# Attention and mixer in one stream: a transpose ahead of its scores, a rank product behind its slot's unit, and the last weight decode two slots later

## The chip, the cores and the metric

One core of a Trainium2 chip. The metric is the device time of one execution in microseconds (us). Engines as in the profile: PE (matmul), PEld (its weight loads, which overlap), DVE, ACT, POOL, SP (issues the transfers).

## What is computed

The output of a causal attention with decay feeds a token mixer of rank 32 and a channel network. B=8, 8 heads, S=576, D=64, width 512, inner width 2048:

```python
scores = scale * q @ k.T + (cum_i - cum_j), masked above the diagonal
attn   = softmax(scores);  o = attn @ v            # per head
x = o as (B, S, 512)
u = x + (x.T @ U @ V).T
out = u + relu(u @ w_ch1) @ w_ch2
```

`cum` is the running sum of log f. All of it is in float32 accuracy. A product is made of float32r parts: the high part is a rounded copy of an operand, the low part the rest; three products (high by high, high by low, low by high) make one.

## The kernel before

**Pairs and steps.** The 64 heads go as 32 pairs p=0..31, four to a batch. `step(t)` takes t=0..33; its ten slots s=0..9 overlap three pairs: p=t gets its scores, the pair before it (a) is transposed and multiplied by V, the pair before that (c) is scaled into x and split. Pairs 0 to 5 run their scores in float32 while the mixer's weights are decoded; from p=6 (`NF`) on in float32r.

**One pair.** Scores of the first head (`S_00` to `S_03`, L418 and L419) stand in slots 0 to 3, the last 64 rows of both heads (`St_0`, `St_1`, L472 and L473) in slots 4 and 5, those of the second head (`S_10` to `S_13`) from the end of slot 6 to slot 9. Each is followed by a maximum on DVE (L439, L477), which yields the bias `nm`, and an exponential on ACT (`P`, L449; `Ptl`, L487). One step later PE transposes `P` (L530; `T_00` to `T_02`, `T_v`, `T_10` to `T_12`), ACT copies the high part (`PTh`, L506), DVE subtracts for the low part (`PTl`, L509), and PE multiplies by V (L642; its operand `VS` is split by ACT at L203 and POOL at L208). Two steps later x is transposed and split (`xT`, `xh`, `xl`), and `ranks` multiplies it by U (`Tt`, L715), after which ACT and DVE copy `TS` (L718, L719, L722).

**Operands of the scores.** `G[0]` and `G[1]` hold q and k of the two heads for p of 6 and more. For each head three casts (L339) write the high parts, then L358 and L359 the low parts of k and of q; `St` reads both heads, its first product G0 alone, the other two G1. Normally ACT and POOL share this. In the pair that follows a mixing step (p=11, 15, 19, 23, 27, 31) all casts of G1 are POOL's.

**Mixer and network.** While attention runs, the steps with p=10, 14, 18, 22, 26 and 30 also run the mixing units of a finished batch: `H`, `Tu` (transposes of u, L780) and `Tv`. u's high part `uh` and low part `ul` are written from PSUM by ACT and DVE; for the last two `Tu` ACT copies the whole (`full`, L755), and POOL writes `uh` (L758) and `ul` (L759) from it. In other steps units of the network, `A` (12 matmuls, L832) or `B` (6 matmuls, L854), stand at the end of a slot, one to a slot as they are due.

**What sets the order.** The order of PE and SP is the order of the code. On ACT, DVE and POOL a scheduler orders the instructions of the attention part; `defer(phase, fn, slots)` says in which later slot, and in what place in it, an instruction is issued to the scheduler, and `behind(ins, kind)` orders one behind the newest of a kind. PSUM: the scores of p of 6 and more alternate between two buffers (`psS`), transposes between two (`psT`), units between two (`psF`); an instruction that writes a buffer waits for the last reader of what was in it.

**The decodes.** The weights come as integers that are decoded on the chip in 14 pieces u=0..13, `DECODES` gives step and slot. The last two (u=12, 13) are halved. The second half of u=13, which belongs to step 7, is issued 3 slots behind its first half, and its first instruction is ordered behind the newest score maximum (`newest["top"]`).

**What touches the change.** In slot 7: `score(p, 1, 1)`, that is `S_11`, stands ahead of `turn_p(a, 1, 1)`, that is `T_11`. In slot 8: `S_12`, `T_12`, `ranks(c)`, that is `Tt`, then the slot's unit.

Of the kernel before, what the change touches and what calls it, by code (L numbers as in the profile page):

```python
# [38 lines left out]
NF = 6  # L39
# [4 lines left out]
def tile_decay_attention_moe(ctx, tc, qk, v, f, U, V, w1, w2, out):  # L44
    nc = tc.nc
# [9 lines left out]
    newest = {}  # L55

    def behind(ins, kind):
        found = newest[kind]
        for x in found if isinstance(found, tuple) else (found,):
            tc.add_manual_dep(  # L60
                ins.ins, x.ins.name,
                mybir.DependencyInfo(mybir.DependencyClass.NoSync, mybir.DependencyReason.DATA), reason=f"order behind {kind}",
            )

    def decode(raw, a, h, l, eng, rows=slice(0, 128), keep=False, sub=nc.gpsimd, low=None, halves=(0, 1)):

        lo, hi = raw[..., 0].bitcast(U32), raw[..., 1]
        af, gf = a.bitcast(F32), hi.bitcast(F32)
        if 0 in halves:
            decode_words(a, af, hi, gf, eng, keep)
        if 1 in halves:
            third = nc.vector.tensor_scalar(hi, a, -0x800000, None, op0=ALU.bitwise_and)
            if 0 not in halves:
                behind(third, "top")
            nc.vector.scalar_tensor_tensor(gf, lo, 2.0**-52, gf, op0=ALU.mult, op1=ALU.mult)
            sub.tensor_tensor(af, af, gf, op=ALU.add)  # L80
            nc.scalar.copy(h, af)
            (low or sub).tensor_tensor(l[rows], af[rows], h.bitcast(F32)[rows], op=ALU.subtract)
# [167 lines left out]
    def decode_w(u, halves=(0, 1)):  # L250
        load_w(u)
        raw, a = staged[u]
        if 1 in halves:
            staged[u] = None
        kind, fc = UNITS[u]
        if kind == "w1":
            h, l = (x[:, fc].rearrange("p c f -> p (c f)") for x in (w1h, w1l))
        elif kind == "w2":
            h, l = w2h[:, fc], w2l[:, fc]
        elif kind == "V":  # L260
            h, l = VV, VV
        else:
            raw = raw.rearrange("p (c r) t -> p c r t", c=NM + 1)
            a = a.rearrange("p (c r) -> p c r", c=NM + 1)
            h, l = Us[:, :, 0:RK], Us[:, :, RK : 2 * RK]
        decode(raw, a, h, l, nc.scalar, slice(96, 128) if kind == "V" else slice(0, 128), keep=True, sub=nc.vector if u not in (0, LATE) else nc.gpsimd, low=nc.vector if 0 < u < LATE else nc.gpsimd, halves=halves)
        if u == len(UNITS) - 1 and 1 in halves:
            nc.gpsimd.memset(xn[NX - 1][64:128, NM, :], 0.0)

# [7 lines left out]
    def defer(phase, fn, slots=1):  # L277
        later.setdefault(now[0] + slots, []).append((phase, fn))
# [6 lines left out]
    def run_filler():  # L285
        w, fn = filler.pop(0)
        fn()
        return w
# [134 lines left out]
    def bank_s(p, name):  # L423

        scored[0] += 1
        if p < NF and scored[0] % 2:
            return psF.tile([P, 512], F32, tag="F", name=name)
        return psS.tile([P, 512], F32, tag="S", name=name)

    def score(p, j, i):  # L430
        z = st[p]
        w = P * (i + 1)
        ps = bank_s(p, f"S{p}_{j}{i}")
        c0 = AMAIN[j] + P * i
        qk_mm(ps[:, :w], p, c0, slice(0, w), True, True, j)
        col = 2 * i + j

        def top():
            ins = newest["top"] = nc.vector.tensor_tensor_reduce(  # L439
                ps[:, :w], ps[:, :w], mask[:, 512 - w : 512], scale=-SCALE, scalar=3.0e38,  # L440
                op0=ALU.add, op1=ALU.min, accum_out=z["nm"][:, col : col + 1],
            )
            if (j, i) == (0, 1) and "joined" in newest:
                behind(ins, "joined")

        def use():
            pt = sb2.tile([P, w], F32, tag=f"P{i}", name=f"P{p}_{j}{i}")
            z["P"][j].append(pt)
            ins = nc.scalar.activation(  # L449
                pt, ps[:, :w], AF.Exp, bias=z["nm"][:, col : col + 1], scale=-1.0, accum_out=z["sm"][:, col : col + 1]  # L450
            )
            if (j, i) == (0, 0):
                newest["exp"] = ins

        defer(0, top)
        defer(2, use)
# [3 lines left out]
    def score_tail(p, x):  # L460
        z = st[p]
        ps = bank_s(p, f"St{p}_{x}")
        cols = slice(hw * x, hw * x + hw)
        if p < NO:
            for j in range(2):
                qk_mm(ps[:, :hw], p, ATAIL[j], cols, j == 0, j == 1, j)
        elif p < NF:
            nc.tensor.matmul(ps[:, :hw], both_q, both_k[:, cols], start=True, stop=True)
        else:
            at = [slice(AOFF[j] + cols.start, AOFF[j] + cols.stop) for j in range(2)]  # L470
            for j in range(2):
                nc.tensor.matmul(ps[:, :hw], G[j][:, 0, ATAIL[j] : ATAIL[j] + P], G[j][:, 2, at[j]], start=j == 0, stop=False)  # L472
            nc.tensor.matmul(ps[:, :hw], G[1][:, 1, 0:P], G[1][:, 3, at[1]], start=False, stop=True)  # L473
        z["tl"].append(ps)

        def top():
            nc.vector.tensor_tensor_reduce(  # L477
                ps[:, :hw], ps[:, :hw], lean[:, hw * x : hw * x + hw], scale=-SCALE,
                scalar=3.0e38 if x == 0 else z["nm"][:, 8:9],
                op0=ALU.add, op1=ALU.min, accum_out=z["nm"][:, 8 + x : 9 + x],  # L480
            )

        def use():
            if x == 1:
                z["ptl"] = sb.tile([P, S], F32, tag="Ptl", name=f"Ptl{p}")
                for y in range(2):
                    newest["tail"] = nc.scalar.activation(  # L487
                        z["ptl"][:, hw * y : hw * y + hw], z["tl"][y][:, :hw], AF.Exp, bias=z["nm"][:, 9:10],
                        scale=-1.0, accum_out=z["sm"][:, 8 + y : 9 + y],
                    )  # L490

        defer(0, top)
        defer(2, use)

# [395 lines left out]
    def held(t):  # L890
        return 4 if t > MIX[-2] else 6
# [42 lines left out]
    LATE = 12  # L934
# [7 lines left out]
    def step(t):  # L942
        p = SEQ[t]
        a, c = (SEQ[t - x] if t >= x else None for x in (1, 2))
        ps_, pa, px = p is not None, a is not None, c is not None
        last, ending = t == LAST, t > LAST - 2
# [7 lines left out]
        for s in range(6 + 2 if last else SLOTS):  # L954
            when = now[0] + 1

            def at(phase, fn):
                later.setdefault(when, []).append((phase, fn))
# [31 lines left out]
            if (t, s) in DECODES:  # L990
                u = DECODES.index((t, s))

                steps = [lambda: load_w(u + (3 if u < 6 else 2)), lambda: decode_w(u)]
                if u < LATE:
                    for fn in steps if u < 8 else steps[::-1]:
                        at(6, fn)
                else:
                    at(6, lambda: decode_w(u, (0,)))
                    defer(6, lambda: decode_w(u, (1,)), 3)
                    defer(6, steps[0], 3)  # L1000
            run_later()
            if s == 4 and ps_ and p > NF:
# [12 lines left out]
            if ps_:  # L1015
                if s < 4:
                    score(p, 0, s)
                elif s < 6:
                    score_tail(p, s - 4)
                elif s > 6:  # L1020
                    score(p, 1, s - 6)
            if px and s == 0:
                values(c, 1)
# [5 lines left out]
                turn_small(a if pa else None, c if px else None)  # L1029
            if pa and s == 5:  # L1030
                turn_tail(a)
            if pa and 6 <= s < 9:
                turn_p(a, 1, s - 6)
            if pa and s == 7:
                values(a, 0)
            if px and s == (6 if last else 8):
                ranks(c)

            if mixing:
                for _ in range(2 if t == MIX[0] and s < 3 else 1):  # L1040
                    mixing.pop(0)[1]()
                for _ in range(1 if ending else (1, 1, 2, 1, 1)[s] if s < 5 else 0):
                    if filler:
                        run_filler()
            elif len(filler) > held(t) and s in ROOM:

                ahead = sum(x >= s for x in ROOM) + len(ROOM) * (min(m for m in MIX if m > t) - 1 - t)
                credit[0] += (len(filler) - held(t)) / max(ahead, 1)
                if credit[0] > 0.999 or t > LAST - 3:
                    credit[0] = max(credit[0] - 1, 0)  # L1050
                    run_filler()
            if ps_ and s == 6:
                score(p, 1, 0)
            if last and s == 7:
# [114 lines left out]
    with tc.manual_schedule(engines={ET.PE, ET.DVE, ET.Activation, ET.SP}):  # L1169
# [12 lines left out]
        h, t = ([fn for _, fn in x] for x in (mixing[0 : NM + 1], mixing[NM + 1 :]))  # L1182
# [622 lines left out]
```

## Time and profile before

| | |
|---|---|
| time, median of 3 runs | 1185.39 us (1185.22 to 1187.29) |
| the profiled execution's own time | 1184.63 us |
| its span | 1182.9 us |
| granted clock of TensorE | 0.999 of full speed |
| busy: PE, PEld, DVE, ACT, POOL | 99%, 91%, 76%, 64%, 50% |

The span is the stretch from the first to the last instruction of the profiled execution; busy shares are shares of it. Attention takes the first 660 us or so, the rest is the network and the last mixing.

### The profile page before, as it was taken

The page shows a single profiled execution, that of the slowest core. Times are in us where ns is not written, and L with a number is a line of the kernel's source. Part 1 is how long each engine was busy: PE and PEld are TensorE (multiplying, and loading weights), DVE is VectorE, ACT ScalarE, POOL GpSimd, SP SyncE. Part 2 cuts the span into 40 slices and gives each one's busy share as a digit, 9 for nine tenths or more (in the row PEclk, how much of TensorE's full clock was granted, in tenths as well). Part 3 has the DMA queues.
Part 4 walks back from the last instruction along what each step waited for, and adds up shares of the span by engine and source line. Part 5 has one row for each costly group of instructions (what it writes and reads, how often), then busy time and mean ns, then how long its engine had stood idle before and what let it go on. Part 6 is the DMA issues. An engine that isn't in the chain of part 4 may idle for free.

```text
span 1182.9 us, 24145 instructions
## 1 busy us (share of the span) xinstructions
PE 1168.8 (99%) x8348; PEld 1074.3 (91%) x8348; DVE 903.0 (76%) x2185; ACT 752.7 (64%) x2046; POOL 594.2 (50%) x668
## 2 busy tenths in 40 slices
PE   9999999999999999999999999999999999999998
PEld 5888899899999989989989987798999999999998
DVE  8987787677777677777686799967776767777675
ACT  8878786766868668867765577344454544544443
POOL 4216766547648458666563000024575555555554
PEclk9999999999999999999999999999999999999999
DMA  5754545536536536546443155352325335243411
GB/s 159 205 151 135 149 121 163 147 98 171 141 98 183 151 86 178 135 112 178 108 129 111 70 163 182 109 143 98 100 90 141 93 124 143 90 117 99 131 49 36
DMA packets 90610, 150.47 MB, mean 127 GB/s; under 512 B 12888, under 2 KB 50264, under 8 KB 88440
## 3 DMA queue, kind: packets, MB, share of 16 engines
q1 hardware_dynamic: 88856, 140.14, 40.4%
q0 software_dynamic: 1152, 8.39, 3.8%
q8 instruction: 66, 1.08, 0.4%
q14 instruction: 56, 0.46, 0.1%
q10 hardware_dynamic: 480, 0.40, 0.1%
HBM read 108.64 MB, written 35.93 MB: 122 GB/s over the span
## 4 chain that ended last, share of the span: by engine, by line
PE 85%; DVE 9%; ACT 3%; issue 1%; DMA 1%; POOL 1%; SPq 0%; DVEq 0%; POOLq 0%; ACTq 0%
PE N L1416 12%; PE B L854 11%; PE A L832 11%; PE A L1396 9%; PE B L1396 7%; PE V L642 6%; PE T L530 4%; PE S L418 3%; PE S L419 2%; PE O L1497 2%; PE B L1416 2%; PE V L607 2%; PE S L415 2%; PE Tt L715 2%; PE O L1260 1%
## 5 line engine op out<-in xcount | busy, mean ns | idle before, releaser
L208 POOL TENSOR_TENSOR hb<-xn,hb 128x256 fp32r<-128x256 f32 x136 | 111.6, 841 | 125.5 <-ACT hb L203 112.9
L449 ACT ACTIVATE P<-S,nm 128x128 f32<-128x128 f32 (+3 forms) x256 | 137.5, 539 | 58.0 <-DVE nm L439 56.0
L439 DVE CUSTOM_DVE_ANT_0 S<-S,mask 128x128 f32<-128x128 f32 (+3 forms) x256 | 125.4, 494 | 52.3 <-PE S L419 41.5
L832 PE MATMUL A<-uh,w1h 128*128 128x256 f32 (+1 forms) x384 | 119.7, 312 | 0.0
L832 PE MATMUL A<-ul,w1h 128*128 128x256 f32 (+1 forms) x384 | 113.6, 296 | 0.0
L832 PE MATMUL A<-uh,w1l 128*128 128x256 f32 (+1 forms) x384 | 113.4, 295 | 0.0
L203 ACT CAST hb<-xn 128x256 fp32r<-128x256 f32 x136 | 51.7, 404 | 84.6 <-DVE xn L1402 45.5
L339 POOL CAST G<-qk 64x576 fp32r<-64x576 f32 (+1 forms) x76 | 50.1, 668 | 89.2 <-PE S L419 56.8
L854 PE MATMUL B<-w2h,hh 128*128 128x512 f32 x216 | 88.2, 408 | 0.0
L509 DVE TENSOR_TENSOR PTl<-T,PTh 128x512 fp32r<-128x512 f32 (+1 forms) x156 | 78.1, 526 | 10.3 <-ACT PTh L506 9.9
L530 PE MATMUL T<-ident,P 128*128 128x128 f32 x544 | 85.3, 272 | 0.0
L854 PE MATMUL B<-w2l,hh 128*128 128x512 f32 x216 | 84.9, 393 | 0.0
L854 PE MATMUL B<-w2h,hl 128*128 128x512 f32 x216 | 84.7, 392 | 0.0
L358 POOL TENSOR_TENSOR G<-qk,G 64x576 fp32r<-64x576 f32 x52 | 74.7, 1437 | 10.8 <-issue 3.8
L1416 PE MATMUL N<-sw,hb 128*128 128x256 f32 x546 | 79.9, 282 | 0.0
L1416 PE MATMUL N<-b2h,hb 128*128 128x256 f32 x420 | 79.8, 282 | 0.0
L359 POOL TENSOR_TENSOR G<-qk,G 64x576 fp32r<-64x576 f32 x52 | 74.9, 1441 | 8.4 <-ACT G L339 7.5
L832 PEld LDWEIGHTS A<-uh,w1h 128*128 128x128 f32 x384 | 72.8, 190 | 0.9 <-DVE hl L837 0.4
L832 PEld LDWEIGHTS A<-uh,w1l 128*128 128x128 f32 x384 | 73.0, 190 | 0.5
L418 PE MATMUL S<-G 128*128 128x128 f32 x208 | 71.4, 348 | 2.0 <-ACT Ptl L487 0.9
L832 PEld LDWEIGHTS A<-ul,w1h 128*128 128x128 f32 x384 | 72.7, 189 | 0.0
L1416 PEld LDWEIGHTS N<-sw,hb 128*128 128x128 f32 x546 | 71.6, 190 | 0.0
(349 smaller groups left out, 3992.6 us busy)
## 6 DMA issues: line engine op xcount, KB each, us to landing
qk<-in_qk_dram SPq DMA_DIRECT2D x104, 288.0 KB
direct<-ud SPq DMA_DIRECT2D x48, 256.0 KB
sr<-in_w_dram SPq DMA_DIRECT2D x20, 512.0 KB
vr<-in_v_dram SPq DMA_DIRECT2D x32, 256.0 KB
ud<-uh SPq DMA_DIRECT2D x32, 256.0 KB
ud<-ul SPq DMA_DIRECT2D x32, 256.0 KB
accd<-ost SPq DMA_DIRECT2D x32, 256.0 KB
xn<-accd SPq DMA_DIRECT2D x8, 1024.0 KB
```

What stands on the lines that cost most here:

```text
L208: return leng.tensor_tensor(dl, src, dh.bitcast(F32), op=ALU.subtract)
L358: low = pin(el.tensor_tensor(g[oth, 2, cols], k[oth], gf[oth, 2, cols], op=ALU.subtract))
L359: last = pin(em.tensor_tensor(g[own, 1, cols], q[own], gf[own, 0, cols], op=ALU.subtract))
L418: nc.tensor.matmul(ps, G[j][:, 0, c0 : c0 + P], G[j][:, 2, cols], start=first, stop=False)
L439: ins = newest["top"] = nc.vector.tensor_tensor_reduce(ps[:, :w], ps[:, :w], mask[:, 512 - w : 512], scale=-SCALE, scalar=3.0e38, op0=ALU. ...
L449: ins = nc.scalar.activation(pt, ps[:, :w], AF.Exp, bias=z["nm"][:, col : col + 1], scale=-1.0, accum_out=z["sm"][:, col : col + 1])
L509: defer(2, lambda: nc.vector.tensor_tensor(dstl, src, dsth.bitcast(F32), op=ALU.subtract))
L530: nc.tensor.transpose(tp[:, P * x : P * x + P], z["P"][j][i][:, P * c : P * c + P], ident)
L832: nc.tensor.matmul(ps[:, :nt], wt[:, fc, c], ut[:, c, sl], start=m == 0, stop=m == 3 * NDC - 1)
L854: nc.tensor.matmul(ps, ht[:, fc, P * x : P * x + P], wt[:, fc], start=fc == 0 and m == 0, stop=fc == NA - 1 and m == 2,)
L1396: nc.tensor.matmul(ps, a[x][:, c], b[y][:, c], start=start and m == 0, stop=m == 5, skip_group_check=not start)
L1416: nc.tensor.matmul(ps[:, y], a[p_][:, P * y : P * y + P], w[q_], start=start and y == 0 and m == 0, stop=stop and y == 1 and m == 2,)
```

## The change

Three edits. First, the second half of the last decode (u=13) is issued 5 slots behind its first half instead of 3, and its first instruction is ordered behind the newest maximum of a tail score (L477) instead of the newest score maximum. Second, in the steps with p of 6 and more, but for the last step, `T_11` comes ahead of `S_11`. Third, `Tt` comes behind the unit of its slot, but for the last step.

```diff
-    def decode(raw, a, h, l, eng, ..., halves=(0, 1)):
+    def decode(raw, a, h, l, eng, ..., halves=(0, 1), after="top"):
...
-                behind(third, "top")
+                behind(third, after)
...
-        decode(..., halves=halves)
+        decode(..., halves=halves, after="top" if u == LATE else "low")
...
         def top():
-            nc.vector.tensor_tensor_reduce(
+            newest["low"] = nc.vector.tensor_tensor_reduce(
...
-                    defer(6, lambda: decode_w(u, (1,)), 3)
+                    defer(6, lambda: decode_w(u, (1,)), 3 if u == LATE else 5)
...
                 elif s > 6:
+                    if s == 7 and pa and p >= NF and not last:
+                        turn_p(a, 1, 1)
                     score(p, 1, s - 6)
...
-            if pa and 6 <= s < 9:
+            if pa and 6 <= s < 9 and not (s == 7 and ps_ and p >= NF and not last):
                 turn_p(a, 1, s - 6)
             if pa and s == 7:
                 values(a, 0)
-            if px and s == (6 if last else 8):
+            if px and last and s == 6:
                 ranks(c)
...
                     run_filler()
+            if px and not last and s == 8:
+                ranks(c)
             if ps_ and s == 6:
                 score(p, 1, 0)
```

The scheduler's order on the other engines differs too. On POOL, at the end of the mixing step of p=14 and the start of p=15 (`full_1` and `full_2` are the copies of the last two `Tu`, `G_91` is G0, `G_92` G1, `mask` the last 64 columns of the tail's mask):

```order
 L339 CAST G_92<-qk_1_3760 128x576 x2
 L339 CAST G_92<-qk_1_3760 64x576
-L758 CAST uh_3738<-full_2_3846 128x4x128
+L382 TENSOR_TENSOR mask<-mask,tri 128x64
 L759 TENSOR_TENSOR ul_3739<-full_1_3811,uh_3738 128x4x128
 L208 TENSOR_TENSOR VS_3983<-vr_3697,VS_3983 128x10x64
+L759 TENSOR_TENSOR ul_3739<-full_2_3835,uh_3738 128x4x128
 L359 TENSOR_TENSOR G_92<-qk_1_3760,G_92 64x576
+L339 CAST G_91<-qk_0_3889 64x576
 L358 TENSOR_TENSOR G_92<-qk_1_3760,G_92 64x576
-L339 CAST G_91<-qk_0_3889 64x576
-L759 TENSOR_TENSOR ul_3739<-full_2_3846,uh_3738 128x4x128
```

The second `ul` moves from behind L358 and the G0 cast to a place ahead of L359, and the G0 cast ahead of L358. The second `uh` cast now stands ahead of the casts of G1, where the mask was, and the mask behind them. It reads alike at p=23 and p=27. At p=11, 19 and 31 the second `ul` stands ahead of `VS` (L208), and the G0 cast stays behind L358.

On DVE, in the second half of the step of p=15 (`PTl` is that of pair 14, `hl` the low part of a unit's result):

```order
 L837 SCALAR_TENSOR_TENSOR hl_0_3932<-A_0_3_4046,hh_0_3931 128x256
+L509 TENSOR_TENSOR PTl_3909<-T_10_4077,PTh_3908 128x512
 L439 ISA S_10_4095,nm_3873<-S_10_4095,mask 128x128
 L439 ISA nm_3873 128x1
-L509 TENSOR_TENSOR PTl_3909<-T_10_4077,PTh_3908 128x512
-L439 ISA S_11_4108,nm_3873<-S_11_4108,mask 128x256
+L837 SCALAR_TENSOR_TENSOR hl_0_3932<-A_0_4_4082,hh_0_3931 128x256
+L439 ISA S_11_4112,nm_3873<-S_11_4112,mask 128x256
 L439 ISA nm_3873 128x1
-L837 SCALAR_TENSOR_TENSOR hl_0_3932<-A_0_4_4082,hh_0_3931 128x256
```

The subtraction of `T_10` moves ahead of the maximum of `S_10`, and `hl` ahead of that of `S_11`.

On ACT, in the first half of the step t=7 (`VS` is that of pair 6, whose load `vr` comes from memory, `stg` and `xn` belong to the decode):

```order
 L842 ACTIVATE hh_0_1456<-A_0_1_1533 128x256
 L87 ACTIVATE stg_1079<-xn_109 128x512
+L203 CAST VS_1572<-vr_1522 128x10x64
 L506 CAST PTh_1506<-T_v 128x256
 L506 CAST PTh_1506<-T_v 128x128
 L449 ACTIVATE P_02_1568,sm_1475<-S_02_1557,nm_1474 128x384
-L203 CAST VS_1572<-vr_1522 128x10x64
 L449 ACTIVATE P_03_1592,sm_1475<-S_03_1575,nm_1474 128x512
```

The cast of `VS` moves from behind `P_02` to a place ahead of both copies of `T_v` and of `P_02`. Further on, in each mixing step, ACT's `full` copy of the last `Tu` moves from behind the `TS` copies to a place ahead of `P_12`.

## Rows read from the trace of the kernel before

**Rows 1.** The page, engines: busy us (share of the span) xinstructions.
```profile
PE 1168.8 (99%) x8348; PEld 1074.3 (91%) x8348; DVE 903.0 (76%) x2185; ACT 752.7 (64%) x2046; POOL 594.2 (50%) x668
```

**Rows 2.** Waits of PE and PEld: us in total, times, longest us.
```profile
PE S L418 <- ACT Ptl L487: 0.9, 1, 0.9
PE Tt L715 <- DVE PTl L509: 0.9, 3, 0.3
...
PEld S L418 <- ACT Ptl L487: 3.5, 15, 1.1
PEld Tt L715 <- DVE PTl L509: 3.4, 11, 0.5
```

**Rows 3.** Timeline of PE, step of p=10: start us, us, instruction.
```profile
195.49 0.39 PE L418 MATMUL S<-G 128*128 128x256 f32 x1
```

**Rows 4.** Timeline of ACT in the same step; [idle before <-releaser].
```profile
192.53 0.58 ACT L449 ACTIVATE P<-S,nm 128x384 f32<-128x384 f32 x1 [0.29 <-DVE nm L439]
...
193.63 0.59 ACT L755 COPY full<-Tu 128x512 f32<-128x512 f32 x1
...
194.66 0.69 ACT L449 ACTIVATE P<-S,nm 128x512 f32<-128x512 f32 x1 [0.17 <-DVE nm L439]
```

**Rows 5.** Timeline of POOL, from the end of p=10 into p=11.
```profile
193.11 0.32 POOL L382 TENSOR_TENSOR mask<-mask,tri 128x64 f32<-128x64 f32 x1 [0.17 <-DVE PTl L509]
193.37 2.00 POOL L339 CAST G<-qk 128x576 fp32r<-128x576 f32 x3
195.44 0.61 POOL L758 CAST uh<-full 128x512 fp32r<-128x512 f32 x1
196.01 1.29 POOL L759 TENSOR_TENSOR ul<-full,uh 128x512 fp32r<-128x512 f32 x1
197.26 1.57 POOL L208 TENSOR_TENSOR VS<-vr,VS 128x640 fp32r<-128x640 f32 x1
...
200.43 1.44 POOL L358 TENSOR_TENSOR G<-qk,G 64x576 fp32r<-64x576 f32 x1
201.82 0.66 POOL L339 CAST G<-qk 64x576 fp32r<-64x576 f32 x1
```

**Rows 6.** Timelines, `St_0` of p=11 (PE) and of p=19 (POOL, PE).
```profile
202.03 0.43 PE L472 MATMUL St<-G 128*128 128x288 f32 x2
202.30 0.29 PE L473 MATMUL St<-G 128*128 128x288 f32 x1
...
367.66 1.44 POOL L358 TENSOR_TENSOR G<-qk,G 64x576 fp32r<-64x576 f32 x1
...
369.13 0.43 PE L472 MATMUL St<-G 128*128 128x288 f32 x2
```

**Rows 7.** Timelines of DVE, ACT and PE, step of p=15.
```profile
295.13 0.30 DVE L439 CUSTOM_DVE_ANT_0 S<-S,mask 128x128 f32<-128x128 f32 x1
...
296.34 0.69 DVE L509 TENSOR_TENSOR PTl<-T,PTh 128x512 fp32r<-128x512 f32 x1 [0.85 <-ACT PTh L506]
...
296.44 0.41 ACT L449 ACTIVATE P<-S,nm 128x128 f32<-128x128 f32 x1
...
301.93 0.68 ACT L449 ACTIVATE P<-S,nm 128x512 f32<-128x512 f32 x1
...
297.00 0.43 PE L418 MATMUL S<-G 128*128 128x384 f32 x1
...
298.22 0.27 PE L715 MATMUL Tt<-xh,Us 128*64 128x128 f32 x1 [0.29 <-DVE PTl L509]
...
302.80 0.36 PE L418 MATMUL S<-G 128*128 128x256 f32 x1
```

**Rows 8.** Timelines of ACT and PE, step t=7.
```profile
119.04 0.62 ACT L449 ACTIVATE P<-S,nm 128x384 f32<-128x384 f32 x1
...
120.03 0.73 ACT L203 CAST VS<-vr 128x640 fp32r<-128x640 f32 x1 [0.27 <-DMA vr<-in_v_dram]
...
119.99 0.43 PE L472 MATMUL St<-G 128*128 128x288 f32 x2
```

More of the change, by code (lines that the diff above doesn't have):

```diff
@@ L63, in behind, with decode @@
             )
-    def decode(raw, a, h, l, eng, rows=slice(0, 128), keep=False, sub=nc.gpsimd, low=None, halves=(0, 1)):
+    def decode(raw, a, h, l, eng, rows=slice(0, 128), keep=False, sub=nc.gpsimd, low=None, halves=(0, 1), after="top"):
         lo, hi = raw[..., 0].bitcast(U32), raw[..., 1]
@@ L265, in decode_w @@
             h, l = Us[:, :, 0:RK], Us[:, :, RK : 2 * RK]
-        decode(raw, a, h, l, nc.scalar, slice(96, 128) if kind == "V" else slice(0, 128), keep=True, sub=nc.vector if u not in (0, LATE) else nc.gpsimd, low=nc.vector if 0 < u < LATE else nc.gpsimd, halves=halves)
+        decode(raw, a, h, l, nc.scalar, slice(96, 128) if kind == "V" else slice(0, 128), keep=True, sub=nc.vector if u not in (0, LATE) else nc.gpsimd, low=nc.vector if 0 < u < LATE else nc.gpsimd, halves=halves, after="top" if u == LATE else "low")
         if u == len(UNITS) - 1 and 1 in halves:
```

## The prediction, made before the changed kernel ran

> **What bounds the kernel now.** I read the page first. PE is busy for 99% of the span and loads weights for 91% of it; every other engine has slack on average, POOL half of the span [rows 1]. So the time is the sum of PE's instructions and of the short waits in between, and a wait ahead of PE is the only thing that a change of order can add or take. Next the groups of waits of PE and its loads: `Tt` waits for `PTl` from DVE 14 times, 0.9 + 3.4 us, and `S` for `Ptl` from ACT 16 times, 0.9 + 3.5 us, together 8.7 us [rows 2]. These are the waits beside which the change puts work. The first question is whether they are worth 8.7, that is whether PE gets ahead for good or meets the same late engine a few slots on. The second is what the new order of ACT, DVE and POOL, which the scheduler made anew, makes late elsewhere; that I took from the order of the two programs, laid over the timelines of before.
>
> **Sum.** It is made against the profiled execution's own 1184.63 us (span 1182.9, the rest lies around it). The median of the runs is 0.76 above it, and I add that at the end.
>
> **Nothing for the swaps themselves.** PE gets no instruction more or less: three transposes and two score matmuls change places in the 26 pairs from p=6 on, and nine `Tt` matmuls and a unit where slot 8 has one. No shape changes. Between back-to-back matmuls of different lines PE shows no gap that depends on which follows which beyond 0.03 us, so the reordering alone is 0.
>
> **The mixing steps (p=10, 14, 18, 22, 26, 30): 0.** Here `Tt` waits 0.23 and `S_11` 0.21, and both go, since each gets other work ahead of it. But look at the end of the same step: `P_13` on ACT starts at 194.66 and takes 0.69, so it ends at 195.35, and `S_01` of the next pair, which needs the PSUM buffer that `P_13` reads, starts at 195.49 [rows 3, 4]. It is 0.14 behind ACT, as close as one engine follows another here. `P_13` waits for DVE's maximum of `S_13`, `P_12` (192.53) for that of `S_12` [rows 4], and both stand in a chain that begins with ACT's copies and DVE's subtractions of the same step, not with PE. What PE wins ahead of `Tt` it therefore loses ahead of `S_01`. The change makes it a little worse: ACT's copy `full<-Tu` of the last mixing unit (193.63, 0.59) now stands ahead of `P_12` instead of behind it, where it fills a gap of 0.29 [rows 4]; worked through, `P_13` ends about 0.1 later. That is swallowed by the next item.
>
> **The steps after them (p=11, 15, 19, 23, 27, 31): +6.7.** Here all the work on G1 lies on POOL, and in the trace of before POOL runs from 193.11 on without a gap [rows 5]: the mask, three casts (2.00), `uh`, `ul`, `VS`, L359, L358. The last L358 starts at 200.43, takes 1.44 and ends at 201.87 [rows 5]. It writes the low part of k into G1. The first product of `St_0` reads G0 alone, the second is the first to read G1. The two start with the row at 202.03 and the third product at 202.30, so the second is at about 202.16 [rows 6]: a slack of 0.29. At p=19 L358 ends at 369.10 and the pair starts at 369.13, its second product at 369.26: 0.16 [rows 6]. Read in this way the six slacks are 0.29, 0.29, 0.16, 0.30, 0.51 and 0.29, in all other pairs 2.8 us and more.
> Now POOL's new order, as the first listing of the change shows it for p=15. The second `uh` cast comes ahead of the casts, at 0.13 (its copy on ACT ends later than POOL gets to it); the mask goes behind them, into the place of that cast: 193.11 to 193.37 is 0.26 for 195.44 to 196.01, 0.57, so -0.31 against the sequence of before. The second `ul` subtraction, which used to stand behind L358 and the G0 cast, comes ahead of L359 and L358: 196.01 to 197.26, 1.25 [rows 5]. So L358 ends 0.13 - 0.31 + 1.25 = 1.07 later. At p=15, 23 and 27 the G0 cast (201.82, 0.66 long, 0.62 to the next start, estimated by the overlaps of neighbouring rows) also comes ahead of L358: 1.69. PE then stands at `St_0`, in order, with the unit and everything else behind it. The stall is the shift less the slack, plus 0.05 for the earlier end of what else is in the way: at p=11, 19 and 31 0.83, 0.96 and 0.83, at p=15, 23 and 27 1.45, 1.44 and 1.23, together 6.74. After it ACT and DVE have caught up, so that shorter waits of the same step go: -0.20 at p=11 and -0.13 at p=19, +0.05 and +0.10 at p=23 and p=25, where other small items turn over: -0.18.
> Bounds: nothing, if POOL starts the stretch earlier by as much as it gets more to do (against this speaks that the casts follow the mask's 193.11 without a gap, and that they overwrite what `S_13` reads until then); and six times 1.69, if all slack is gone, 10.1. I take the rows.
>
> A place where the Trainium skill looks the other way is "Perfetto Trace Analysis", section Identifying the Most-Contended Engine: optimise the engine with the highest occupancy first, and for TensorE judge by the busy share of its weight loads, then find and remove its gaps. That engine is PE by this trace too (91% of loads), and by that rule the gaps removed at `Tt` and `S` would be the change's worth and POOL at 50% nobody's concern. The rows on POOL say that an engine at half load is 0.29 us from holding PE in six places.
>
> **DVE at p=15: +0.65.** The order puts the subtraction `PTl<-T_10` ahead of the maximum of `S_10`. That maximum was at 295.13; `PTl` starts only at 296.34, since it waits for ACT, and takes 0.69 [rows 7]. The maximum then ends at about 297.3, its `P_10` (was 296.44, 0.41) at 297.8, and `S_12`, which needs the buffer, starts at 297.95 instead of 297.00: +0.95 [rows 7]. `Tt`'s wait of this step (0.29 on the row at 298.22, with the load's 0.53) goes in turn, so `S_13` is late by 0.45; then `P_13`, which ACT started at 301.93 for 0.68, comes behind `TS` and the casts of G and ends near 303.3, and `S_01` (was 302.80) starts near 303.45: +0.65 [rows 7]. Bounds: 0, if DVE catches up before `S_01`, and 0.95.
>
> **ACT at t=7: +0.2.** The cast `VS<-vr` (120.03, after 0.27 of waiting for the load of `vr`) now stands ahead of `PTh<-T_v` and of `P_02`, which ran at 119.04 [rows 8]. ACT executes in order, so `P_02` starts at 121.06 at the earliest (120.03 + 0.73, less the overlap of neighbours, and the copies of `T_v` that lie between) and ends 0.62 later at 121.68; `St_0` of pair 7 takes over the buffer and moves from 119.99 to 121.83: +1.84 [rows 8]. Against that the first edit gets the last w2 decode out of DVE's and ACT's way: it is 2 slots later, so the wait of `S` for `Ptl` at 125.68 (0.9 on the matmul [rows 2], 1.05 with its load) goes, and about 0.6 of waiting at the next values. Net +0.2, between -0.9 and +0.94 (-1.6 if `vr` lands early, for the order of SP's transfers is unchanged).
>
> Sum: 1184.63 + 0 + 6.74 - 0.18 + 0.65 + 0.2 = 1192.04 of own time, **1192.8 us** against the median.
>
> **Rivals.** (A) PE keeps what it wins. All 8.7 us of waits go and nothing becomes late, because POOL and DVE have time on average: 1184.63 - 8.7 + 0.76 = 1176.7. That is what the rule named above comes to; for it speaks the load of POOL, against it the 0.14 between `P_13` and `S_01` and the six slacks. It is decided by L358: if it ends before `St_0`'s second product, the loss of 6.7 is gone. (B) POOL isn't late (the casts start earlier, or `ul` waits less), but the mixing steps give their gains back and t=7 and p=15 cost what I say: 1184.63 + 0.65 + 0.2 + 0.5 of small items + 0.76 = 1186.8, which can't be told from no change. (C) The loss is larger: the G0 cast at p=15, 23 and 27 stands and waits for PE (it needs the buffer that the scores of before still read), and holds L358 behind it, or t=7 costs its upper bound: 1196 and more.
>
> **Numbers.** Chances: the forecast 0.65, A 0.10, B 0.17, C 0.08. The forecast's own range is 1190 to 1194.5 (p=15 at 0 to 0.95, t=7 at -0.9 to +0.94, slacks within 0.1 each). The range takes in B with half of its width and the nearer part of C: 1184.5 to 1196; A and what lies beyond stay out. A measurement of this kernel tells 0.2%, 2.4 us, from no change. Faster by more has A and a little of B, 0.13; within it most of B and the lowest tail of the forecast, 0.19; slower by more 0.68.
>
> **What would show it.** Right: `St_0` (L472) waits for POOL's G (L358) in six steps, 0.8 to 1.5 us each, at p=11, 15, 19, 23, 27 and 31; the waits of `Tt` for `PTl` are gone and `S_01` in the mixing steps waits for `P_13` as before; `S_12` at p=15 waits about 1 us; at t=7 `St_0` waits for `P_02`, and `S_10` no longer for `Ptl`. Wrong: no wait of `St_0` for POOL (then A or B), or one of several us (C). The prediction falls if POOL's stretch begins earlier than 193.1 relative to the step's scores, for everything large in it hangs on that one chain.

## The result, and the profile after

| | before | after |
|---|---|---|
| time, median (lowest to highest) | 1185.32 us (1184.77 to 1187.29), 6 runs | 1193.37 us (1192.86 to 1197.27), 6 runs |
| ratio to before | | 1.0073, 95% interval 1.0057 to 1.0088 |
| profiled execution, span | 1182.9 us | 1191.3 us |

The change makes the kernel 8 us slower. The page's line of engines, of after, to be read beside [rows 1]: POOL is as busy as before, in half of the span.

```profile
PE 1167.9 (98%) x8348; PEld 1073.0 (90%) x8348; DVE 904.7 (76%) x2185; ACT 755.5 (63%) x2046; POOL 594.0 (50%) x668
```

The waits of PE and of its loads, of after, in the columns of [rows 2]:

```profile
PE S L418 <- ACT P L449: 5.2, 12, 1.0
PE St L472 <- POOL G L358: 4.1, 5, 1.2
...
PE St L472 <- DMA vr<-in_v_dram: 1.2, 1, 1.2
PE St L472 <- ACT P L449: 0.8, 1, 0.8
...
PEld St L472 <- POOL G L358: 6.6, 6, 1.4
PEld S L418 <- ACT P L449: 5.9, 14, 1.3
```

`Tt` no longer stands in it and `S` hardly waits for `Ptl`: the waits aimed at are gone. In their place `St` waits for POOL in six places, and `S` waits 12 times for the exponentials `P` on ACT: three times at t=7, six times at the start of the pair behind a mixing step, and at p=8, 15 and 25. (The wait put down to a load, `vr`, is p=23's `St_0`. The load is named as the last of several. L358 ended there at 462.37 and the product that waited started at 462.43, so it is POOL's too.)

The timeline of POOL and then of PE at the start of p=11, of after, the place of [rows 5] and [rows 6]:

```profile
194.15 1.17 POOL L758 CAST uh<-full 128x512 fp32r<-128x512 f32 x2
195.27 2.01 POOL L339 CAST G<-qk 128x576 fp32r<-128x576 f32 x3
197.36 0.32 POOL L382 TENSOR_TENSOR mask<-mask,tri 128x64 f32<-128x64 f32 x1
197.64 2.55 POOL L759 TENSOR_TENSOR ul<-full,uh 128x512 fp32r<-128x512 f32 x2
200.15 1.58 POOL L208 TENSOR_TENSOR VS<-vr,VS 128x640 fp32r<-128x640 f32 x1
201.80 1.43 POOL L359 TENSOR_TENSOR G<-qk,G 64x576 fp32r<-64x576 f32 x1
203.31 1.42 POOL L358 TENSOR_TENSOR G<-qk,G 64x576 fp32r<-64x576 f32 x1
...
203.90 0.29 PE L472 MATMUL St<-G 128*128 128x288 f32 x1
204.78 0.40 PE L472 MATMUL St<-G 128*128 128x288 f32 x1 [0.58 <-POOL G L358]
```

Both `uh` and both `ul` now run ahead of L358. It ends at 204.73, and the second product of `St_0` starts 0.05 later, 0.88 behind the first; the usual distance is 0.13. PE loses 0.75 here, 0.83 was forecast. By the same reading the six places lose 0.75, 1.26, 0.76, 1.36, 1.34 and 0.77, 6.2 us.

The end of the mixing step of p=10, ACT and then PE, of after, the place of [rows 3, 4]:

```profile
193.90 0.62 ACT L755 COPY full<-Tu 128x512 f32<-128x512 f32 x1
194.38 0.62 ACT L449 ACTIVATE P<-S,nm 128x384 f32<-128x384 f32 x1
...
196.53 0.69 ACT L449 ACTIVATE P<-S,nm 128x512 f32<-128x512 f32 x1 [0.66 <-DVE nm L439]
...
195.23 0.30 PE L418 MATMUL S<-G 128*128 128x128 f32 x1 [0.36 <-ACT P L449]
...
197.37 0.38 PE L418 MATMUL S<-G 128*128 128x256 f32 x1
```

The copy stands ahead of `P_12`, and `S_00` of the next pair (195.23) now waits 0.36 for `P_12`. `S_01` starts 0.15 behind the end of `P_13` (196.53 + 0.69), as it did before by 0.14, and both come 1.9 later than before, all but 0.1 of it lost in earlier steps. What PE won at `Tt` and `S_11` it lost here, at `S_00` already.

Step t=7, of after, on ACT, PE, DVE and POOL, the place of [rows 8]; the last two lines are those of before, for the two DVE instructions:

```profile
120.61 0.74 ACT L203 CAST VS<-vr 128x640 fp32r<-128x640 f32 x1
...
121.65 0.63 ACT L449 ACTIVATE P<-S,nm 128x384 f32<-128x384 f32 x1
...
122.42 0.53 PE L472 MATMUL St<-G 128*128 128x288 f32 x2 [0.84 <-ACT P L449]
...
131.50 0.44 PE L418 MATMUL S<-G 128*128 128x384 f32 x1 [1.02 <-ACT P L449]
...
122.05 2.56 DVE L93 SCALAR_TENSOR_TENSOR stg<-stg,xn 128x512 int32<-128x512 int32 x1
...
128.56 1.87 DVE L80 TENSOR_TENSOR stg<-stg,xn 128x512 f32<-128x512 f32 x1
...
122.51 1.56 POOL L208 TENSOR_TENSOR VS<-vr,VS 128x640 fp32r<-128x640 f32 x1
...
128.46 1.43 POOL L359 TENSOR_TENSOR G<-qk,G 64x576 fp32r<-64x576 f32 x1 [0.30 <-ACT G L339]
...
121.14 0.67 DVE L93 SCALAR_TENSOR_TENSOR stg<-stg,xn 128x512 int32<-128x512 int32 x1
...
125.20 0.68 DVE L80 TENSOR_TENSOR stg<-stg,xn 128x512 f32<-128x512 f32 x1
```

`St_0` waits for `P_02`, as forecast. But `S_12` (131.50) waits 1.02 for `P_10` too. That is behind two instructions of the decode on DVE, L93 and L80, that take 2.56 and 1.87 us here and 0.67 and 0.68 in the same step before. The last section comes back to them.

### The profile page after: what moved, and what is told of

The parts are those of the page before. It is cut to its first block, busy times and chain, and to the rows that moved or that the text cites. A ratio compares the mean times of both kernels' runs of the same rounds, so it can differ in the third digit from the quotient of the medians.

```text
span 1191.3 us, 24191 instructions
## 1 busy us (share of the span) xinstructions
PE 1167.9 (98%) x8348; PEld 1073.0 (90%) x8348; DVE 904.7 (76%) x2185; ACT 755.5 (63%) x2046; POOL 594.0 (50%) x668
## 5 line engine op out<-in xcount | busy, mean ns | idle before, releaser
L208 POOL TENSOR_TENSOR hb<-xn,hb 128x256 fp32r<-128x256 f32 x136 | 111.7, 841 | 125.4 <-ACT hb L203 112.8
L339 POOL CAST G<-qk 64x576 fp32r<-64x576 f32 (+1 forms) x76 | 50.5, 674 | 88.1 <-PE S L419 54.7
L358 POOL TENSOR_TENSOR G<-qk,G 64x576 fp32r<-64x576 f32 x52 | 74.6, 1435 | 10.3 <-issue 4.1
L359 POOL TENSOR_TENSOR G<-qk,G 64x576 fp32r<-64x576 f32 x52 | 74.8, 1439 | 6.7 <-ACT G L339 4.9
```

Source lines behind the costliest of these rows:

```text
L208: return leng.tensor_tensor(dl, src, dh.bitcast(F32), op=ALU.subtract)
L358: low = pin(el.tensor_tensor(g[oth, 2, cols], k[oth], gf[oth, 2, cols], op=ALU.subtract))
L359: last = pin(em.tensor_tensor(g[own, 1, cols], q[own], gf[own, 0, cols], op=ALU.subtract))
```

## The experiments

The theory: PE's new order is harmless, and the loss is made by a few instructions on POOL and ACT that the scheduler, given the new order, let pass in front of something that PE waits for; the largest is POOL's at the six starts. The rival: a part of the change costs by itself on PE. First the parts one at a time, then the orderings put back one at a time. All medians stand beside runs of before on the same chip, with a median of 1185.1 to 1185.2. The intervals are 1.0 to 1.5 us wide to either side, so differences of a few tenths between two runs tell nothing.

| | what | median us | ratio to before, 95% interval |
|---|---|---|---|
| e1 | decode's move alone | 1185.21 | 1.0001 (0.9992 to 1.0010) |
| e2 | turn of `T_11` and `S_11` alone | 1188.01 | 1.0026 (1.0016 to 1.0037) |
| e3 | `Tt` behind the unit alone | 1190.54 | 1.0047 (1.0034 to 1.0059) |
| e4 | all, POOL pinned | 1187.95 | 1.0025 (1.0015 to 1.0034) |
| e5 | all, copy behind `P_12` | 1187.35 | 1.0017 (1.0007 to 1.0027) |
| e9 | e5, and `VS` behind `P_02` | 1185.22 | 0.9995 (0.9985 to 1.0004) |
| e8 | e9, and `PTh` behind `P_10` | 1183.01 | 0.9978 (0.9967 to 0.9989) |
| e6 | e2, and `VS` behind `P_02` | 1186.16 | 1.0008 (0.9997 to 1.0018) |
| e10 | e6, and `PTh` behind `P_10` | 1185.98 | 1.0005 (0.9995 to 1.0016) |
| e7 | decode's move and `Tt`, copy behind `P_12` | 1182.27 | 0.9969 (0.9957 to 0.9981) |

**e1, the decode's move alone.**

```diff
-                behind(third, "top")
+                behind(third, after)
...
-                    defer(6, lambda: decode_w(u, (1,)), 3)
+                    defer(6, lambda: decode_w(u, (1,)), 3 if u == LATE else 5)
```

> The decode's move alone, the rest as before. POOL keeps its order at the starts of the pairs behind mixing steps, and ACT keeps VS behind P_02 at t=7. Theory (POOL's order is the loss): the 1.05 us wait of S_10 at t=7 and about 0.6 at the values go, a part of them is given back at S_12: 1184.0 to 1185.4, that is -1.3 to +0.1 us against before. Rival (the decode's move itself costs what the changed kernel loses at t=7): +1 us, 1186.3.

It is 1185.21, in its range, and no change that can be told. The profiled execution shows the gain: PE is 1.0 us ahead of before from t=7 on, of which 0.24 are there at p=6 already, ahead of the edit. It keeps that until p=27, where it loses 0.7 of it. At p=19 it loses 0.3 and has it back by the end of the step. The mask on POOL at p=19, then the mask, L358 and `St_0` at p=27:

```profile
359.60 0.32 POOL L382 TENSOR_TENSOR mask<-mask,tri 128x64 f32<-128x64 f32 x1 [0.61 <-DMA mask<-based]
...
526.98 0.32 POOL L382 TENSOR_TENSOR mask<-mask,tri 128x64 f32<-128x64 f32 x1 [0.99 <-DVE TS L722]
...
534.35 1.42 POOL L358 TENSOR_TENSOR G<-qk,G 64x576 fp32r<-64x576 f32 x1
...
535.07 0.29 PE L472 MATMUL St<-G 128*128 128x288 f32 x1
535.83 0.40 PE L472 MATMUL St<-G 128*128 128x288 f32 x1 [0.46 <-DMA vr<-in_v_dram]
```

L358 ends at 535.77, and the second product starts 0.06 behind it. POOL's order is that of before here, and in that order the mask opens POOL's stretch. The mask waits for the load of its data, by name at p=19; at p=27 the profile names a subtraction on DVE, but before ran the mask ahead of that subtraction, and here as at p=19 the last packets of the load end 0.6 ahead of the mask. So it is the late load that takes the slack, not PE's lead: with the same lead the slack at p=11, 15 and 23 is 0.34 to 0.41, more than before, and in e2, where PE is 1.9 behind, the mask waits 0.97 at p=15 and `St_0` 0.41 after it. In before too the mask's wait and the slack behind it add up to about the same: 0.17 and 0.29 at p=11, 0.31 and 0.16 at p=19, 0 and 0.51 at p=27. In the changed kernel's order the mask stands behind the casts, and this wait is gone.

**e2, the turn alone.**

```diff
                 elif s > 6:
+                    if s == 7 and pa and p >= NF and not last:
+                        turn_p(a, 1, 1)
                     score(p, 1, s - 6)
...
-            if pa and 6 <= s < 9:
+            if pa and 6 <= s < 9 and not (s == 7 and ps_ and p >= NF and not last):
```

> T_11 ahead of S_11 alone. POOL keeps its order at the six starts; ACT takes VS ahead of P_02 at t=7, DVE takes PTl<-T_10 ahead of the maximum of S_10 at p=15. Theory: no wait of St_0 for POOL; +1 us at t=6 and t=7, +0.5 at p=15, the 0.2 us waits of S_11 in the mixing steps are given back at the tail of the same step: 1185.5 to 1187.5. Rival (what PE wins it keeps): eight waits of 0.2 us go for good, 1183.7.

1188.01, 0.5 above the range and far from the rival. The longest wait is that of `St_0` for `P_02` at t=7, 1.89; from p=6 to p=8 PE loses 1.4 us. In the mixing steps `S_11` waits less, but the weight load of `Tt` waits 0.56 instead of 0.22: the wait moved on by one place.

**e3, `Tt` behind the unit alone.**

```diff
-            if px and s == (6 if last else 8):
+            if px and last and s == 6:
                 ranks(c)
...
+            if px and not last and s == 8:
+                ranks(c)
             if ps_ and s == 6:
```

> Tt behind its slot's unit alone. POOL's order turns over at all six starts, and at five of them the G0 cast too stands ahead of L358. Theory: St_0 waits for POOL's L358 in six steps, 1.45 + 1.45 + 1.58 + 1.44 + 1.23 + 0.83 = 8.0 us by the slacks of before; Tt's waits of 0.3 to 0.5 us at p=11, 15, 19 and 23 go, 1.9 us, of which half may be kept: 1191.4 to 1193.3. Rival (the loss comes from the three parts together or from elsewhere on PE): within 2 us of before.

1190.54, 5.5 us slower, 0.9 below the range and far from the rival. Six waits of `St_0` for L358 by themselves turn up, 1.31, 1.31, 1.33, 1.31, 1.22 and 0.73, 7.2 us; about 2 us of gain at `Tt` and the steps behind it stand against them. So this part alone makes POOL's new order. The three parts apart add up to 0.1 + 2.9 + 5.5 = 8.5 us, together they cost 8.05.

**e4, the changed kernel with POOL pinned.**

```diff
-                    nc.gpsimd.tensor_tensor(dl, whole, dh.bitcast(F32), op=ALU.subtract)
+                    ins = nc.gpsimd.tensor_tensor(dl, whole, dh.bitcast(F32), op=ALU.subtract)
+                    if late == 2:
+                        behind(ins, "lows")
...
-        pin(copy(ek2, g[own, 3, cols], k[own]))
+        own_k = pin(copy(ek2, g[own, 3, cols], k[own]))
+        if j == 0 and p - 2 in MIX[1:]:
+            behind(own_k, "lows")
```

> The changed kernel with two orderings on POOL and nothing else: the second ul subtraction and the G0 cast of the next pair stand behind the low parts of G1 (L358, L359) again. L358 then ends 0.2 us earlier than before. Theory: the waits of St_0 for POOL go, 6.2 us by the changed kernel's trace (0.75 + 1.26 + 0.76 + 1.36 + 1.34 + 0.77), and nothing takes their place: 1186.3 to 1187.5. Rival (PE is held by ACT and DVE anyway, so that the wait turns up behind St_0): 1190 and more.

1187.95, 0.5 above the range: 5.4 us of the 8.05 come back, by an edit of POOL's order that moves nothing on PE. No wait of `St_0` for POOL is left. A part of it turns up again behind it: `S_12` of p=11, 15, 19 and 23 waits 0.3 to 0.5 us longer, so the rival is right for that much.

**e5, the copy behind `P_12`.**

```diff
+            newest["exp", j, i] = ins
...
-                defer(3, lambda: nc.scalar.copy(whole, src))
+                def copy_whole():
+                    ins = nc.scalar.copy(whole, src)
+                    if late == 2:
+                        behind(ins, ("exp", 1, 2))
+                defer(3, copy_whole)
```

> The changed kernel with one ordering, on ACT: the whole copy of the last Tu of a batch stands behind P_12 of its step, as before. POOL isn't touched, but the scheduler then puts the second uh and ul on POOL back behind the low parts of G1 by itself. Theory (the root of POOL's new order is that Tt behind the unit lets this copy come one place earlier on ACT): the waits of St_0 for POOL go and the 0.1 us in each mixing step too; 1186.3 to 1188.2. Rival (POOL's order has another root, Tt's place itself): St_0 still waits, 1192 or more.

1187.35, in the middle of the range. The timeline of POOL and PE at p=11, of e5:

```profile
198.66 1.43 POOL L359 TENSOR_TENSOR G<-qk,G 64x576 fp32r<-64x576 f32 x1
200.17 1.58 POOL L208 TENSOR_TENSOR VS<-vr,VS 128x640 fp32r<-128x640 f32 x1
201.71 1.43 POOL L358 TENSOR_TENSOR G<-qk,G 64x576 fp32r<-64x576 f32 x1
...
203.72 1.27 POOL L764 TENSOR_TENSOR ul<-full,uh 128x512 fp32r<-128x512 f32 x1
...
203.48 0.43 PE L473 MATMUL St<-G 128*128 128x288 f32 x2
```

(`newest["exp", j, i]` keeps each exponential for `behind`; the runs that follow have this line too.) The second `ul` is behind L358 again, which ends 0.34 ahead of `St_0`. So the root of the six waits is one place on ACT: `Tt` behind the unit makes `Tu` earlier, its copy gets ahead of `P_12`, so the scheduler takes `uh` and `ul` earlier on POOL, and L358 has to wait behind them.

**e6, the turn with `VS` behind `P_02`, and e10, with `PTh` behind `P_10` as well.**

```diff
-... "exp" if p == NF + 1 else None)
+... "exp" if p == NF + 1 else ("exp", 0, 2) if p == NF else None)
```

> T_11 ahead of S_11 alone (1188.0 by itself) with one ordering: the cast of VS of pair 6 stands behind P_02 at t=7, as before. Theory: the 2.05 us wait of St_0 for P_02 at t=7 goes, a part of it returns at S_10 and S_12 of that step: 1186.4 to 1187.0. Rival (the loss of this part sits in every step, since the copy PTh of T_11 now stands ahead of P_10 on ACT and S_12 waits for P_10): 1187.6 or more.

```diff
-    def evac(dsth, dstl, src):
-        defer(0, lambda: nc.scalar.copy(dsth, src))
+    def evac(dsth, dstl, src, late=False):
+        def high():
+            ins = nc.scalar.copy(dsth, src)
+            if late:
+                behind(ins, ("exp", 1, 0))
+        defer(0, high)
...
-                evac(z["PTh"][:, j, sl], z["PTl"][:, j, sl], src)
+                evac(z["PTh"][:, j, sl], z["PTl"][:, j, sl], src, (j, g) == (1, 1))
```

> T_11 ahead of S_11 alone (1188.0), with VS of pair 6 behind P_02 (1186.2) and PTh of T_11 behind P_10 in every step. Theory: the turn's cost is that copy on ACT, and with it back the waits of Tt in the mixing steps fall from 0.60 to 0.2 or so and those of S_12 at p=11, 15, 19, 23 by half: 1183.3 to 1185.0. Rival (the turn on PE costs by itself, since Tt comes nearer to T_11): 1186 as without the ordering.

e6 is 1186.16, 0.2 below its range: 1.9 of the turn's 2.9 us are that one cast at t=7. e10 is 1185.98, 1.0 above its range: putting `PTh` back gives the turn alone nothing that can be told. The waits of `Tt`, of e10:

```profile
PE Tt L720 <- DVE PTl L514: 3.0, 9, 0.4
...
PEld Tt L720 <- PE T L535: 6.5, 15, 0.6
```

`Tt` still stands right behind `T_12`, and its waits on PE grow from six (2.1 us) in e6 to nine (3.0 us): what `S_12` no longer waits, `Tt` does. The rival holds in this form: without the third part the turn brings nothing. (In the profiled executions of e6 and e10 0.6 us of the loss are at p=27, where the mask on POOL waits 1.0 to 1.1, as in e1.)

**e7, without the turn.** The edits of e1, e3 and e5.

> The decode's move and Tt behind the unit, without the turn of T_11 and S_11, with the whole copy behind P_12. Theory: no wait of St_0 for POOL; Tt's waits of 0.3 to 0.5 us at p=11, 15, 19 and 23 are kept as a gain of about 1 us, the mixing steps give 0: 1184.0 to 1185.5. Rival (nothing won at Tt is kept): 1185.1 as before, which this can hardly tell apart; or Tt's place costs something without POOL: 1186 and more.

1182.27, 1.7 us below the range: more was to be had at `Tt` than I gave it. It beats before by 2.8 us and the changed kernel by 11, and has the lowest median of all; from e8 the intervals don't tell it apart. The waits of PE and of its loads, of e7:

```profile
PE S L418 <- ACT P L449: 1.2, 3, 0.8
...
PEld S L418 <- ACT P L449: 2.9, 9, 1.0
PEld S L418 <- ACT Ptl L488: 2.2, 13, 0.2
```

From p=6 on `Tt` and `St` wait for nothing. By the start times of its scores beside before's, 0.7 us come at t=7, and 0.2 to 0.5 in each of the steps of p=11, 15, 19, 23 and 25. Each of the mixing steps gives less than 0.15.

**e8 and e9, all parts with three and with two orderings put back.** Edits of e5 and e6 (e9), and of e10 (e8).

> All three parts with three orderings on ACT put back: the whole copy behind P_12, VS of pair 6 behind P_02 at t=7, and PTh of T_11 behind P_10 in every step. Theory (the whole loss is work of ACT and POOL that the scheduler let pass in front of something PE waits for; the order of PE is harmless): 1184.0 to 1186.0. Rival (the turn of T_11 and S_11 on PE costs by itself): 1187 or more.

> The changed kernel with two of the three orderings: the whole copy behind P_12 and VS of pair 6 behind P_02 at t=7, but PTh of T_11 left where the scheduler put it. Against the two neighbours (1187.35 with the copy alone, 1183.01 with all three) it says what each is worth. Theory (t=7 costs 1.4 to 1.7 us by the traces, PTh ahead of P_10 the rest): 1185.4 to 1186.0, so 2.4 to 3 us for PTh. Rival (nearly all of the 4.3 us lies at t=7): 1183.5 or less.

e9 is 1185.22, 0.2 below its range and equal to before. e8 is 1183.01, 1.0 below its range. What the third ordering does at p=11, on ACT and PE, of e9:

```profile
208.54 0.49 ACT L507 CAST PTh<-T 128x384 fp32r<-128x384 f32 x1
208.90 0.40 ACT L449 ACTIVATE P<-S,nm 128x128 f32<-128x128 f32 x1
...
209.45 0.45 PE L418 MATMUL S<-G 128*128 128x384 f32 x1 [0.63 <-DVE hl L842]
```

and of e8:

```profile
208.56 0.38 ACT L449 ACTIVATE P<-S,nm 128x128 f32<-128x128 f32 x1
208.90 0.50 ACT L508 CAST PTh<-T 128x384 fp32r<-128x384 f32 x1
...
209.08 0.44 PE L418 MATMUL S<-G 128*128 128x384 f32 x1 [0.25 <-ACT P L449]
```

In e9 `S_12` starts 0.15 behind the end of `P_10` (208.90 + 0.40), so it is `P_10` that it waits for, though the row names `hl`; with `P_10` ahead of the copy it starts 0.37 earlier.

The chain changed kernel, e5, e9, e8 splits the loss by one ordering at a time: 1193.37, 1187.35, 1185.22, 1183.01. The copy ahead of `P_12` (and through it POOL) costs 6.0 us, `VS` ahead of `P_02` 2.1, `PTh` ahead of `P_10` 2.2. With all three put back the parts are worth 2.1 us against before. PE's order is the same in all four. The last two steps are not much larger than the intervals; the start times of the scores in the four traces give 1.7 at t=7 for `VS` and 2.3 over the later steps for `PTh`. The prices hold for this sequence: in the changed kernel itself `S_12` of p=11, 19 and 23 isn't held by `P_10`, since POOL has already made PE late there; that wait turns up only when POOL's is gone.

## Why the prediction was right, point by point

The time (1192.8 forecast, 1193.37 measured), the sign and the main mechanism were right; that the sum came out 0.6 from the measured time is luck, since terms that it had wrong cancel.

- **The steps after the mixing steps, +6.7: right.** The places were the six named, the waits 0.75 to 1.36 (forecast 0.83 to 1.45), 6.2 in sum. Taken away, they give 5.4 (e4), or 6.0 with their root on ACT (e5). The order of POOL and the slack were enough to work this out. The differences by slack did not come, though: the waits measure 0.75 to 0.77 at p=11, 19 and 31 and 1.26 to 1.36 at p=15, 23 and 27. The six slacks of before differ by how long the mask waited in that execution (e1), and in the new order the mask no longer opens the stretch.
- **The mixing steps, 0: right.** `S_01` stands 0.15 behind `P_13` as before. What was won is lost one score sooner than forecast, at `S_00`, which waits for `P_12` behind the copy.
- **"DVE at p=15: +0.65": too large.** `S_12` of p=15 comes 0.5 later against before than `S_10` of that pair (forecast 0.95), and at `S_01` of p=16 0.2 of it are left.
- **"ACT at t=7: +0.2": mis-sized.** In the changed kernel PE loses 1.6 us between p=6 and the end of p=8, and regains 0.3 at p=9. `VS` ahead of `P_02` is worth 2.1 us (e5 to e9), 1.9 in the turn alone (e2 to e6). That the waits at 125.68 and at the next values go holds for e1, where PE wins 0.7 at t=7, but with `VS` moved the decode's L93 and L80 also meet POOL's instructions and hold `P_10` back.
- **A term was left out:** `T_11` ahead of `S_11` lets `PTh` pass in front of `P_10`, and `S_12` waits for `P_10`'s buffer. The sum priced it at p=15 only (+0.65, and through DVE). Over all steps it costs 2.2 us where `Tt` has moved too (e9 to e8).
- **"-0.18" for what goes in later steps: mis-sized the other way.** In the changed kernel PE regains 0.4, 0.4 and 0.3 behind `St_0` of p=11, 19 and 23, where 0.33 in all was forecast. With the orderings put back, the waits removed at `Tt` are kept for the most part behind the mixing steps: 2.1 us (e8) to 2.8 us (e7, which has the decode's gain in it too).
- **Rival A**, PE keeps what it wins, fails as a forecast of this kernel; of the gaps that it counts, 2.1 us (e8) and 2.8 us (e7, with the decode's gain in it) were to be had. Its 8.7 us are too many to begin with. They add PE's waits to those of its loads, and the four of PE are the same stalls as four of the loads: 0.29 and 0.52 at the `Tt` of p=15, 0.90 and 1.10 at 125.68. Counted once it is 6.9. The rule of the Trainium skill ("Perfetto Trace Analysis", Identifying the Most-Contended Engine and Optimization Strategy: optimise the engine with the highest occupancy, find its gaps) points at gaps that are really there. But in this case an engine at 50% cost PE 6 us, so beside that rule the order of the other engines had to be read here.

What stays open: why the mask's load comes late at p=27 in e1, e6 and e10 and not in before; there is one profile of each. And why `PTh` behind `P_10` is worth 2.2 us with `Tt` behind the unit and 0.2 without it is argued from `Tt`'s waits, not tried apart.

## What to carry to other kernels

Where a scheduler orders some engines, an edit of the hand-written order of one engine is an edit of all: compare the order of every engine, and for each instruction that passes another, look up the slack of the one passed. An engine at half load can be as critical as the busiest one: here its chain ended 0.2 to 0.5 us ahead of its reader. When such an edit loses, put the passed instructions back one by one before giving up the edit: here three orderings turned +8.0 us into -2.1 (e8), and one ordering without the turn into -2.8 (e7).

## What the runs showed of the hardware

Two instructions of the decode on DVE, L80 and L93, which read two operands in SBUF, took much longer beside POOL's work on SBUF, and POOL's beside them. L80 takes 0.68 us undisturbed. In the changed kernel POOL's L359 started at 128.46, L80 at 128.56, and L80 took 1.87, ending 0.54 after L359. In e9 the order is the other way round, DVE and then POOL:

```profile
126.43 0.68 DVE L80 TENSOR_TENSOR stg<-stg,xn 128x512 f32<-128x512 f32 x1
...
126.55 1.86 POOL L359 TENSOR_TENSOR G<-qk,G 64x576 fp32r<-64x576 f32 x1 [0.30 <-ACT G L339]
```

Here L80 takes its 0.68, and L359 is the one that is late: 1.86 instead of 1.43. Of these two, whichever came first ran at its own speed; e1 has it as e9 (0.68 and 1.96). The Trainium skill says so ("SBUF — State Buffer", Who interferes with whom): a VectorE instruction with two SBUF inputs contends with a GpSimd instruction that reads SBUF, over ports that they share and that are an exclusive lock, and issue order decides who blocks. For L80 and L359 the traces agree. L93 is less plain. In the changed kernel it started at 122.05, while POOL's cast L339 ran from 121.67 to 122.53; `VS` on POOL followed at 122.51, after L93, and still took only 1.56, while L93 took 2.56 and ended 0.54 after `VS`. Held up behind one instruction of POOL, it was passed by the next. In e2, with the same three side by side, L93 took 1.03 and `VS` 1.99. With `VS` put back (e9) L93 takes 0.68.

For this kernel it means that a DVE instruction that comes to stand beside another one of POOL can become longer by 1.2 us (L80) or 1.9 us (L93), which no sum over durations of before would show. No run keeps the two engines apart.
